# Attention followed by a mixture of experts: the first 128 rows of expert 0 selected by TensorE while the routing still runs

## The chip, the cores and the metric

The kernel runs on one core of a Trainium2 chip. The metric is the device time of one launch in microseconds (us). TensorE is called PE in the profile, VectorE DVE, ScalarE ACT, GpSimd POOL; SP is the engine whose queue starts most of the DMAs.

## The reference

Attention with pooled queries gives 1152 token rows of 512 numbers. A gate chooses one of 8 experts for each token. Expert e takes the first 288 of its tokens in the order of the tokens; each goes through two matrices, 512 to 1024 and 1024 to 512, with a relu between, and the result is scaled by the gate's probability.

```python
q_pool = q.reshape(B, H, S // factor, factor, D).mean(axis=3)       # B, H, S, D = 2, 8, 1152, 64
scores = scale * np.matmul(q_pool, k.transpose(0, 1, 3, 2))
attn = np.exp(scores - np.max(scores, axis=-1, keepdims=True))
attn = attn / (np.sum(attn, axis=-1, keepdims=True) + 1e-09)
x = np.matmul(attn, v).transpose(0, 2, 1, 3).reshape(N, D)          # N, D = 1152, 512
...
expert_idx = np.argmax(x @ w_gate, axis=1)
for i in range(N):
    e = expert_idx[i]
    if counts[e] < capacity:                                        # capacity = 288
        disp[e, counts[e]] = x[i]; pos[i] = counts[e]; counts[e] += 1; keep[i] = True
h = np.maximum(np.einsum('ecd,edf->ecf', disp, w1), 0.0)
y = np.einsum('ecf,efd->ecd', h, w2)
out[i] = gate_w[i] * y[expert_idx[i], pos[i]]                       # for the tokens kept
```

## The kernel before

**Attention.** Eight pairs of heads (four for each of the two batches) go through PE one after the other; a pair has 27 rounds of scores (`s`), exponentials (`p`), transposes (`tp`) and products with the values (`pv`, from a value tile `vraw` that has two buffers). A finished group of a pair is turned into token rows in `x_out` (tile `xps`, then `x_tok` in SBUF and gate products in `lp`). The order on PE is the order in which the code is written; DVE's order in the last rounds is a scheduler's.

**Routing.** `route(b, t0, t1)` works on tiles of 128 tokens. The last batch's tokens come in three pieces: tiles 0 and 1, tiles 2 and 3, and tile 4 (half full). Each piece is some 15 small DVE operations, with two small matmuls on PE between them that count the tokens of the same expert ahead (`rps`). The outcome is `slot`, an integer row number e * 288 + rank for every token. POOL then writes every token row to that row of `xs`, a tensor in device memory, by an indirect DMA (L551, "scatter"), one for each tile of 128 tokens. `classes` counts the tokens of each expert (`cps`) into flags `more_i`, by which the code later branches.

**Filler.** Behind the counts PE has eight matmuls of 128x512 (tile `warm`, L763; the profile shows each as two), whose result nothing uses.

**Experts.** The rows of expert e come back from `xs` into `xe` (`load_x`, L795): expert 0's on SP's queue, the others' on POOL's. `trans_x` turns 128 of them over on PE (`xps`, L802), ACT copies that into `xf` (L803), and a `unit` of 64 places follows: up (`hps`, 32 matmuls, L890), relu, turn over (`htp`), down (`yps`, 32 matmuls, L930), scaling by the gate (`yo`, L822, which needs the gate column that `tags` copies out of `xe` on POOL), and a scatter to the output (L828). An expert with more places has further units of 64, 128 and 32 behind branches (`later`, L950); a branch hint for them is issued behind each up half. `trans_x` of the next expert lies inside the unit. The eight experts run in order on PE.

**Weights.** An expert's weights are four chunks of 1 MB. Sixteen chunk buffers `wraw0` to `wraw15` exist: 0 to 5 from the start, 6 to 15 in memory that attention's tiles leave. SP's queue is in order: chunks 6 to 12, then expert 0's rows, then chunks 13 to 15, and then one for each buffer that comes free.

## Time and profile before

| what | us |
|---|---|
| median of 3 runs (lowest, highest) | 488.81 (488.57, 491.68) |
| profiled execution, its own time | 491.99 |
| its span from the first to the last instruction | 490.3 |
| PE busy in the span | 449.8 |
| mean granted TensorE clock, share of full speed | 0.974 |

The span is 1.7 us shorter than the execution's own time. A time in the profile counts from the span's start. PE is the engine to follow; the other engines' busy shares average over an attention part (up to about 306 us), where all of them work, and an expert part, where PE works nearly alone.

### The profile page before, as it was taken

Reading aid. Unit: us, or ns where it says so; the run is one execution under the profiler, and the core shown is the slowest. Engines: PE = TensorE matmul, PEld = TensorE weight load, DVE = VectorE, ACT = ScalarE, POOL = GpSimd, SP = SyncE. Lnnn points to the kernel's source line nnn. Section 1 sums busy time; section 2 is a strip of 40 time slices with the busy share of each in tenths; the row PEclk is TensorE's granted clock in tenths of the full one; section 3 lists DMA queues with packets and bytes.
Section 4 is the critical chain, followed back from the end, with each engine's and each line's share of the span. In section 5 each row is a group of like instructions: output and inputs, shape, how many; then the busy total and the mean of one; then the engine's idle time right before and its main releaser. Section 6 shows DMA issues by size and latency. Waiting matters only on the chain. (4 is left out here: it accounts for less than half of the span.)

```text
span 490.3 us, 9116 instructions
## 1 busy us (share of the span) xinstructions
PE 449.8 (92%) x3183; PEld 315.5 (64%) x3183; DVE 245.9 (50%) x725; ACT 251.1 (51%) x731; POOL 170.9 (35%) x290
## 2 busy tenths in 40 slices
PE   4779999999999999999999998996999999999990
PEld 3667777777677677677776765464668456674670
DVE  5687777777777999887777565010100011001100
ACT  5777887787787677777777761020221112101100
POOL 4477444344344454454433001522031133112110
PEclk9799999999999999999999999798999999999996
DMA  7998984033043044052104625699983093000000
GB/s 216 276 284 282 385 285 108 5 98 100 5 98 102 1 119 124 3 150 55 30 20 139 260 70 204 215 341 355 363 285 145 5 364 123 13 12 24 12 11 21
DMA packets 55737, 69.96 MB, mean 143 GB/s; under 512 B 21873, under 2 KB 32117, under 8 KB 55680
## 3 DMA queue, kind: packets, MB, share of 16 engines
q1 hardware_dynamic: 50320, 53.56, 35.5%
q0 software_dynamic: 4816, 15.66, 8.5%
q8 instruction: 32, 0.52, 0.4%
q14 instruction: 25, 0.20, 0.1%
q10 hardware_dynamic: 544, 0.02, 0.1%
HBM read 52.48 MB, written 11.98 MB: 131 GB/s over the span
## 5 line engine op out<-in xcount | busy, mean ns | idle before, releaser
L376 DVE TENSOR_REDUCE negm<-s 128x1 f32<-128x384 f32 x216 | 119.6, 554 | 56.9 <-PE s L371 55.8
L371 PE MATMUL s<-k,q 128*128 128x384 f32 x432 | 132.8, 390 | 9.6 <-ACT p L392 9.0
L392 ACT ACTIVATE p<-s,negm 128x384 f32<-128x384 f32 x216 | 125.0, 587 | 14.6 <-DVE negm L380 9.2
L409 PE MATMUL tp<-ident,p 128*128 128x128 f32 x648 | 106.8, 274 | 0.5 <-DVE pt L418 0.4
L371 PEld LDWEIGHTS s<-k,q 128*128 128x128 f32 x432 | 66.8, 194 | 45.3 <-ACT p L392 25.2
L409 PEld LDWEIGHTS tp<-ident,p 128*128 128x128 f32 x648 | 83.9, 141 | 10.0 <-issue 1.4
L420 ACT COPY pt<-tp 128x384 f32<-128x384 f32 (+1 forms) x160 | 69.3, 445 | 38.5 <-PE tp L409 35.5
L434 PE MATMUL pv<-pt,vraw 128*64 128x256 f32 (+2 forms) x612 | 85.4, 403 | 0.8 <-ACT xt L442 0.8
L273 POOL TENSOR_TENSOR q<-qts,q 64x256 fp32r<-64x256 f32 (+1 forms) x76 | 52.0, 693 | 55.0 <-DVE q L267 47.8
L229 POOL TENSOR_TENSOR k<-kts,k 64x384 fp32r<-64x384 f32 x42 | 44.8, 1068 | 53.7 <-DVE k L228 51.9
L890 PE MATMUL hps<-wraw,xf 128*64 128x256 f32 (+1 forms) x448 | 49.7, 390 | 8.1 <-PEq L950 4.6
L828 POOL DMA_INDIRECT out_dram<-yo,id x17 | 17.1, 1006 | 112.9 <-issue 42.5
L434 PEld LDWEIGHTS pv<-pt,vraw 128*64 128x64 f32 x612 | 36.3, 136 | 27.2 <-issue 10.6
L930 PE MATMUL yps<-wraw,ht 128*64 128x256 f32 (+1 forms) x448 | 48.1, 382 | 1.2 <-DVE ht L907 1.2
L895 DVE TENSOR_SCALAR hs<-hps 128x256 f32<-128x256 f32 x12 | 5.1, 425 | 87.9 <-PE hps L890 87.9
L890 PEld LDWEIGHTS hps<-wraw,xf 128*64 128x64 f32 (+1 forms) x448 | 30.5, 136 | 26.5 <-issue 7.5
L392 ACT ACTIVATION_READ_ACCUMULATOR p<-s,negm 128x1 f32 x216 | 44.5, 206 | 0.0
L418 DVE COPY pt<-tp 128x384 f32<-128x384 f32 (+1 forms) x80 | 40.0, 508 | 6.1 <-PE tp L409 6.0
L822 ACT ACTIVATE yo<-yps,gt 128x256 f32<-128x256 f32 (+1 forms) x15 | 7.7, 516 | 61.5 <-PE yps L930 31.1
L930 PEld LDWEIGHTS yps<-wraw,ht 128*64 128x64 f32 (+1 forms) x448 | 28.4, 133 | 16.8 <-ACT ht L909 1.8
L849 PEld LDWEIGHTS hps<-xf,wraw 128*128 128x128 f32 x192 | 21.7, 192 | 1.2 <-issue 1.2
L849 PE MATMUL hps<-xf,wraw 128*128 128x128 f32 x192 | 22.2, 277 | 0.0
(117 smaller groups left out, 377.0 us busy)
## 6 DMA issues: line engine op xcount, KB each, us to landing
wraw<-in_moe_w_dram SPq DMA_DIRECT2D x32, 1024.0 KB, 7.9
vraw<-in_v_dram SPq DMA_DIRECT2D x8, 576.0 KB, 4.0
kc<-k SPq DMA_DIRECT2D x16, 288.0 KB, 4.0
xs<-zrow POOLq DMA_DIRECT2D x4, 1032.0 KB
qraw<-in_q_dram SPq DMA_DIRECT2D x16, 256.0 KB, 3.6
kraw<-in_k_dram SPq DMA_DIRECT2D x14, 288.0 KB, 4.6
xe<-xs POOLq DMA_DIRECT2D x14, 258.0 KB, 6.0
out_dram<-zrow POOLq DMA_DIRECT2D x2, 1024.0 KB
```

What stands on the lines that cost most here:

```text
L229: nc.gpsimd.tensor_tensor(out=tl[rl, c], in0=kt_s[rh, :], in1=f32(tl[rh, c]), op=ALU.subtract)
L273: nc.gpsimd.tensor_tensor(out=tl[r0, 1, c], in0=qt_s[rs, a:z], in1=f32(tl[rs, 0, c]), op=ALU.subtract)
L371: nc.tensor.matmul(ps[:, 0:CW], a, w, start=i == 0, stop=i == len(terms) - 1)
L376: nc.vector.tensor_reduce(out=negm3[g][:, j:j + 1], in_=ps[:, 0:CW], axis=AX.X, op=ALU.max, negate=True)
L392: nc.scalar.activation(pexp[g][:, j * CW:(j + 1) * CW], sthird.pop(n)[:, 0:CW], AF.Exp, bias=negm3[g][:, 3:4], scale=1.0, accum_out=sums[p ...
L409: nc.tensor.transpose(ps[:, i * P:(i + 1) * P], pexp[g][:, kt * P:(kt + 1) * P], ident)
L418: nc.vector.tensor_copy(dst, sr)
L420: nc.scalar.copy(dst, sr)
L434: nc.tensor.matmul(ps[j * D:(j + 1) * D, 0:n], vraw[:, j, kt, :], pts[p, j, src][:, kt, c0:c0 + n], start=kt == 0, stop=kt == KT - 1,)
L849: at = nc.tensor.matmul(ps[:, i * n:(i + 1) * n], raw[c][:, d, i * P:(i + 1) * P], xf[:, d, o:o + n], start=d == 0, stop=d == DC - 1,)
L890: at = nc.tensor.matmul(ps[g * n:(g + 1) * n, 0:256], xf[:, d, o:o + n], raw[c // 512][:, d, c % 512:c % 512 + 256], start=d == 0, stop=d ...
L930: nc.tensor.matmul(ps[k:k + n, 0:256], ht[:, j, g * n:(g + 1) * n], raw[2 + r // 512][:, r % 512 // P, c * 256:(c + 1) * 256], start=i == ...
```

## The change

Expert 0's first 128 rows no longer take the way over `xs` and `xe` to PE. They are made on PE by matmuls with 0/1 matrices:

- DVE compares column numbers 0 to 127 (`col_i`) with a token's `slot` and writes a 128x128 matrix of zeros and ones for each tile of the last batch (`early["sel"]`). A matmul of the token rows (`x_tok`) with it puts each token's row, turned over already, into the column of its place. Tokens of other experts have slots of 288 and more and give columns of zeros.
- The rows that the first batch left in `xs` are loaded into SBUF during the last pair of heads (`load_early`, on SP's queue) and added by a matmul with the identity.
- Both the loaded rows and the 0/1 matrices lie in one tile that takes the buffer of a value tile no longer used.
- `pick` writes the matmuls, four for each tile, into one PSUM tile (`xsel`). The loaded rows and tile 0 come behind round 32 of the last pair, tile 1 behind round 33, tiles 2 to 4 behind the counts. After the last ACT copies the sum to `xf_first`, which the first two units of expert 0 use.
- The eight `warm` matmuls are gone, and so is expert 0's first `trans_x`. Expert 0's rows are still loaded, for gates, row numbers and later units.
- SP loads the first block of expert 1's rows, then expert 0's three, then the rest of expert 1's; POOL keeps experts 2 and up. In unit 0 of expert 0, five empty steps push `trans_x` of expert 1 to the end of the down half, and the flags are read behind the first up half and no more ahead of the unit.

```diff
+    col_i = const.tile([P, P], I32, name="col_i")
+    nc.gpsimd.iota(col_i, pattern=[[1, P]], base=0, channel_multiplier=0)
+    xf_first = const.tile([P, DC, P], F32, name="xf_first")
...
     nc.vector.memset(lp, 0.0)
+    nc.vector.memset(x_tok[MIX:P, B - 1, QT, 0:DM], 0.0)
...
             tc.add_to_no_dep_group("place", ins.ins)
+        if b == B - 1:
+            nc.vector.tensor_tensor(
+                out=early["sel"][:, t0:t1], in0=col_i.unsqueeze(1).to_broadcast([P, nt, P]),
+                in1=slot[:, t0:t1].unsqueeze(2).to_broadcast([P, nt, P]), op=ALU.is_equal,
+            )
...
+    def load_early():
+        t = lt_p.tile([P, 2, KT, D], F32, tag="vraw", name="early", bufs=2).rearrange("p a t d -> p (a t d)")
+        early["x"], early["sel"] = t[:, 0:DM], t[:, DM:DM + NT * P].rearrange("p (t c) -> p t c", c=P)
+        nc.sync.dma_start(out=early["x"], in_=xs[0:P, 0:DM])
+
+    def pick(*which):
+        if "ps" not in early:
+            early["ps"] = s_ps.tile([P, 512], F32, tag="s", name="xsel")
+        ps = early["ps"]
+        for t in which:
+            x, w = (early["x"], ident) if t < 0 else (x_tok[:, B - 1, t, 0:DM], early["sel"][:, t])
+            for d in range(DC):
+                nc.tensor.matmul(
+                    ps[:, d * P:(d + 1) * P], x[:, d * P:(d + 1) * P], w,
+                    start=t < 0 and d == 0, stop=t == QT and d == DC - 1, skip_group_check=True,
+                )
+            if t == QT:
+                nc.scalar.copy(xf_first, ps.rearrange("p (d c) -> p d c", c=P))
...
+        PICK = {32: (-1, 0), 33: (1,)}
...
+                    if p == NP - 1 and i == 12:
+                        load_early()
...
-        routed = classes().ins
-
-
-        warm = m_ps.tile([P, 512], F32, tag="t", name="warm")
-        for _ in range(8):
-            nc.tensor.matmul(warm[:, 0:512], ident, wraw[0][:, 0], start=True, stop=True)
+        with tc.manual_schedule(engines={mybir.EngineType.PE}):
+            classes()
+            pick(2, 3, QT)
...
-    def load_x(e):
-        q = nc.gpsimd if e else nc.sync
-        for s, c in blocks:
+    def load_x(e, part=slice(None)):
+        q = nc.gpsimd if e > 1 else nc.sync
+        for s, c in blocks[part]:
...
-        xf = xfs[e % 2]
+        xf = xf_first if e == 0 and o < P else xfs[e % 2]
...
+        load_x(1, slice(0, 1))
+        load_x(0)
+        load_x(1, slice(1, None))
+        for e in range(2, min(NX, E)):
             load_x(e)
...
-        trans_x(0, 0)
         for e in range(E):
-            nxt = [lambda: trans_x(e + 1, 0), lambda: flags_of(e + 1)] if e + 1 < E else ()
-            unit(e, 0, nxt, hint(e, 1, flags[e]))
+            nxt = [lambda: trans_x(e + 1, 0), lambda: flags_of(e + 1)] if e + 1 < E else []
+            if e:
+                unit(e, 0, nxt, hint(e, 1, flags[e]))
+            else:
+                unit(0, 0, [lambda: None] * 5 + nxt, first_hint)
```

What this makes of the orders, at three places. First PE, from the routing's matmuls to expert 0 (`rps` are the counts of the three pieces, `cps` that of all, `hps` the first up matmul). Before:

```order
L523 MATMUL rps_3901<-oh_3870,upper_69 128x16
L524 MATMUL rps_3901<-tot_2569,ones_72 128x16
L523 MATMUL rps_3942<-oh_3908,upper_69 128x16
L524 MATMUL rps_3942<-tot_3898,ones_72 128x16
L523 MATMUL rps_3955<-oh_3921,upper_69 128x8
L524 MATMUL rps_3955<-tot_3937,ones_72 128x8
L564 MATMUL cps_3982<-tot_3949,ones_72 128x8
L763 MATMUL warm_3989<-wraw0_153,ident_63 128x512 x8
L957 TENSOR_LOAD more_i_100
L802 MATMUL xps_4089<-ident_63,xe0_4042 128x128 x4
L890 MATMUL hps_4099<-wraw0_153,xf0_4045 64x256
```

And after, on the same engine from the same matmul on:

```order
L528 MATMUL rps_3907<-oh_3876,upper_69 128x16
L529 MATMUL rps_3907<-tot_2573,ones_72 128x16
L593 MATMUL xsel_3949<-ident_63,early_3659 128x128 x4
L593 MATMUL xsel_3949<-early_3659,x_tok_107 128x128 x4
L528 MATMUL rps_3958<-oh_3914,upper_69 128x16
L529 MATMUL rps_3958<-tot_3904,ones_72 128x16
L593 MATMUL xsel_3949<-early_3659,x_tok_107 128x128 x4
L528 MATMUL rps_3975<-oh_3927,upper_69 128x8
L529 MATMUL rps_3975<-tot_3944,ones_72 128x8
L574 MATMUL cps_4006<-tot_3965,ones_72 128x8
L593 MATMUL xsel_3949<-early_3659,x_tok_107 128x128 x12
L921 MATMUL hps_4112<-wraw0_157,xf_first_83 64x256
```

Twelve selections stand between the counts of the pieces, twelve behind the last count, and the `warm` matmuls and expert 0's transposes are gone ahead of the first up matmul.

Second DVE, at the slots of the last two pieces (`slot_3910` and `slot_3916` are tiles 2 and 3, the next `slot` is tile 4). Before:

```order
L548 TENSOR_TENSOR slot_3910<-r1_3909 128x2
L532 TENSOR_SCALAR r1_3922<-r1_3922 128x1
L539 TENSOR_SCALAR r1_3922<-r1_3922 128x1
L567 TENSOR_SCALAR cl_3984<-cps_3982 128x8
L533 RECIPROCAL x_tok_104<-r1_3922 128x1
L543 SCALAR_TENSOR_TENSOR slot_3923<-r1_3922 128x1
L567 TENSOR_SCALAR cl_3984<-cps_3982 128x8 x2
L568 CAST more_i_100<-cl_3984 128x24
```

And after:

```order
L553 TENSOR_TENSOR slot_3916<-r1_3915 128x2
L567 TENSOR_TENSOR early_3659<-col_i_81,slot_3916 128x256
L539 TENSOR_TENSOR rt_3926<-rps_3975,oh_3927 128x8
L577 TENSOR_SCALAR cl_4008<-cps_4006 128x8
L543 TENSOR_REDUCE r1_3928<-rt_3926 128x1
L577 TENSOR_SCALAR cl_4008<-cps_4006 128x8
L544 TENSOR_SCALAR r1_3928<-r1_3928 128x1
L577 TENSOR_SCALAR cl_4008<-cps_4006 128x8
L548 SCALAR_TENSOR_TENSOR slot_3929<-r1_3928 128x1
L578 CAST more_i_103<-cl_4008 128x24
L567 TENSOR_TENSOR early_3659<-col_i_81,slot_3929 128x128
```

The comparison for tiles 2 and 3 stands ahead of tile 4's last steps, and tile 4's own is the last operation; the comparison for tiles 0 and 1 stands some twenty rows further up.

Third SP's queue, from chunk 11 to the first chunks of expert 3 (`xe0` and `xe1` are the rows of experts 0 and 1). Before:

```order
L620 DMA wraw11_4037<-in_moe_w2_dram 128x4x512
L620 DMA wraw12_4038<-in_moe_w1_dram 128x4x512
L795 DMA xe0_4042<-xs_68 128x516 x2
L795 DMA xe0_4042<-xs_68 32x516
L620 DMA wraw13_4039<-in_moe_w1_dram 128x4x512
L620 DMA wraw14_4040<-in_moe_w2_dram 128x4x512
```

And after:

```order
L649 DMA wraw11_4066<-in_moe_w2_dram 128x4x512
L649 DMA wraw12_4067<-in_moe_w1_dram 128x4x512
L826 DMA xe1_4072<-xs_68 128x516
L826 DMA xe0_4071<-xs_68 128x516 x2
L826 DMA xe0_4071<-xs_68 32x516
L826 DMA xe1_4072<-xs_68 128x516
L826 DMA xe1_4072<-xs_68 32x516
L649 DMA wraw13_4068<-in_moe_w1_dram 128x4x512
```

One block of expert 1 stands ahead of expert 0's rows now, and two more ahead of chunk 13; further up in the same queue the new load of the first batch's rows stands directly ahead of chunk 6.

## Rows read from the trace of the kernel before

**Rows 1.** The page, busy time and share of the span.

```profile
span 490.3 us, 9116 instructions
PE 449.8 (92%) x3183; PEld 315.5 (64%) x3183; DVE 245.9 (50%) x725; ACT 251.1 (51%) x731; POOL 170.9 (35%) x290
```

**Rows 2.** Timeline, routing to expert 0: start, duration, instructions [idle before, releaser].

```profile
301.63 0.41 DVE L479 TENSOR_TENSOR x_tok<-xps,z 128x256 f32<-128x256 f32 x1
...
301.97 0.17 DVE L473 TENSOR_TENSOR lp<-xps,z 64x16 f32<-64x16 f32 x1
...
303.43 0.15 DVE L548 TENSOR_TENSOR slot<-r 128x2 int32<-128x2 f32 x1
...
304.34 1.02 POOL L551 DMA_INDIRECT xs<-x_tok,slot  x1 [10.90 <-DVE r L512]
...
305.32 10.17 PE L763 MATMUL warm<-wraw,ident 128*128 128x512 f32 x16
...
306.08 0.22 DVE L543 SCALAR_TENSOR_TENSOR slot<-r 128x1 int32<-128x1 f32 x1
...
309.51 0.91 POOL L551 DMA_INDIRECT xs<-x_tok,slot  x1 [0.30 <-issue]
...
311.95 1.29 SPq L795 DMA_DIRECT2D xe<-xs  x3
...
315.33 0.60 PE L802 MATMUL xps<-ident,xe 128*128 128x128 f32 x4
...
315.71 0.18 POOL L812 COPY gt<-xe 64x1 f32<-64x1 f32 x1
...
316.01 0.58 ACT L803 COPY xf<-xps 128x512 f32<-128x512 f32 x1 [11.09 <-PE xps L802]
...
316.65 3.67 PE L890 MATMUL hps<-wraw,xf 128*64 128x256 f32 x32 [0.72 <-ACT xf L803]
```

**Rows 3.** Busy time by stage: PE, PEld, DVE, ACT, POOL, granted clock, DMA share, GB/s.

```profile
302.00:303.00 1.00, 0.20 (x2) 0.10 (x1) 1.00 (x10) 0.00 (x0) 0.00 (x0) 1.00 1.04 401
...
304.00:305.00 1.00, 0.53 (x4) 0.47 (x3) 0.84 (x10) 0.21 (x1) 0.66 (x1) 0.83 0.03 8
...
311.00:312.00 1.00, 1.00 (x3) 0.32 (x2) 0.00 (x0) 0.00 (x0) 0.00 (x0) 0.76 0.18 46
```

**Rows 4.** Timeline of PE alone, experts 0 to 3.

```profile
325.64 3.67 PE L890 MATMUL hps<-wraw,xf 128*64 128x256 f32 x32 [0.69 <-ACTq L950]
...
338.52 5.36 PE L890 MATMUL hps<-wraw,xf 128*64 128x256 f32 x32 [4.58 <-PEq L950]
...
357.33 3.67 PE L890 MATMUL hps<-wraw,xf 128*64 128x256 f32 x32 [0.74 <-ACTq L950]
```

**Rows 5.** The line of the branches, PE's alone: ns min/median/max, first and last start.

```profile
L950 PEldq COMPARE_BRANCH  x19: 65/183/6457, 322.6 to 479.4; - x19
```

**Rows 6.** The line that reads the flags, PE's alone: ns min/median/max.

```profile
L957 PEldq TENSOR_LOAD <-more_i x8: 772/781/1265, 306.7 to 416.4; - x8
```

**Rows 7.** Timeline of SP's DMA issues, the first of chunks 6 and up.

```profile
264.76 1.68 SPq L620 DMA_DIRECT2D wraw<-in_moe_w_dram  x3
```

**Rows 8.** Timeline of PE, the last value products of pair 6.

```profile
275.28 1.83 PE L434 MATMUL pv<-pt,vraw 128*64 128x320 f32 x12
```

**Rows 9.** Busy time by stage in the first pair, columns as in Rows 3.

```profile
26.00:28.00 2.00, 0.67 (x5) 0.61 (x5) 1.93 (x4) 1.37 (x4) 1.85 (x4) 1.00 0.99 350
```

**Rows 10.** Timeline of the start.

```profile
1.99 0.59 DVE L109 MEMSET lp<- 128x640 f32 x1 [0.18 <-issue]
...
4.97 0.76 DVE L200 TENSOR_TENSOR qp<-qraw 128x256 f32<-128x256 f32 x2 [2.38 <-DMA qraw<-in_q_dram]
```

**Rows 11.** DMA issues, KB each, median us to landing.

```profile
xe<-xs POOLq DMA_DIRECT2D x14, 258.0 KB, 6.0
...
xe<-xs SPq DMA_DIRECT2D x2, 258.0 KB, 2.9
```

## The prediction

> **What bounds the kernel now.** I read the page first: PE is busy 92% of the span [rows 1], so only places where PE does nothing useful can give time. Then the timeline from the routing to expert 0 [rows 2], because the change works there and nowhere else. Expert 0's first up matmul starts at 316.65. Followed back: ACT's copy at 316.01, the transposes at 315.33, SP's load of expert 0's rows at 311.95, the fifth scatter at 309.51, the first at 304.34 (five scatters one behind the other, some 1.3 us each), and the last slot, ready at 306.08 + 0.22 = 306.30. PE's rows in this stretch are only filler: 16 `warm` records over 10.17 us. So 316.65 - 306.30 = 10.35 us lie between the moment at which every place is known and the first useful matmul, and nearly all of it is the way over device memory. After 316.65 I read PE alone [rows 4]: the units follow each other with gaps of 0.69 and 0.74 behind a branch, and one of 4.58. No gap there is a wait for weights. So a microsecond won ahead of expert 0 stays won, unless a gap behind it grows.

> The third view is the clock by stage [rows 3]. [...]

> **The change part by part.**

> *Removed: the way over memory.* The last slot, the comparison for tile 4, four matmuls, ACT's copy, then expert 0. No row shows the comparison; the nearest is the 128x256 operation on DVE at 301.63, which takes 0.41 us and lets the next start 0.34 us later [rows 2]. Two comparisons of that width stand ahead of the last slot: 0.68 us if all of it is added, nothing if DVE's waits for PE swallow it. PE's selections ahead of the last counts can hold up those counts by a few tenths more. I take 0.7: last slot at 307.0, with 306.3 and 307.4 as ends. The half-width comparison of tile 4 with its hand-off, 0.3 to 0.4 us, brings PE to 307.4. The last four selections have the shape of the four transposes at 315.33, and from there to the first up matmul the trace shows 316.65 - 315.33 = 1.32 us, ACT's copy included [rows 2]. **At full clock expert 0 starts at 307.4 + 1.32 = 308.7**, 7.95 us earlier. At half clock the twelve selections behind the last count take twice as long, 1.2 us for each four where 0.60 is shown. They can start when tiles 2 and 3 are compared, about 306.4, and end between 308.8 and 310.0; near the lower end, since two groups overlap, 309.1. With the 0.72 us from there to the up matmul **expert 0 starts at 309.8**, 6.85 us earlier.

> *Lost: the filler.* [...] Where `warm` ran, the clock came back 6.2 us after steady work began, a loss of half of that, 3.1 us. Behind the 4.58 us gap the up half took 5.36 us and not 3.67, a loss of 1.69 us [rows 4]. I take the middle, 2.4.

> *Moved: the next expert's transposes* go to the end of expert 0's down half, so ACT's 0.58 us copy now stands directly ahead of `yo`, on whose end PE's next unit waits (the 0.69 us gap is released by ACT's queue [rows 4]). Part of it overlaps the last matmuls; I charge 0.2 us, with 0 and 0.58 as ends.

> *Moved: the flag load.* It now sits between the up halves of expert 0 on PE. It takes 772 ns at least [rows 6], but for the other experts it already lies inside the down half, which takes the same 3.67 us as an up half without one; nothing, and 0.8 us if that cover fails.

> *Moved on SP.* The new load waits for pair 6's last value products, which end at 275.28 + 1.83 = 277.1 [rows 8]. Behind it in the queue stand chunks 6 and up, now issued from 264.76 [rows 7]; they start 12 us later. Expert 1 needs chunk 6 only after 317, so this costs nothing; were it to cost, PE would show a wait in expert 1's down half. The three more issues ahead of chunk 13 are 0.43 us each (three in 1.29 us [rows 2]); expert 3 starts at 357.33 [rows 4]. Nothing. Expert 1's first block leaves first, lands 2.9 us behind 311.95 [rows 11], and is wanted around 316 at the earliest.

> *Added at the start.* A memset on DVE like the 0.59 us one there lies ahead of a wait of 2.38 us for the first load [rows 10]; a small GpSimd table likewise. Nothing.

> **The sum.** With the clock at half: 6.85 - 2.4 - 0.2 = 4.25 us. The profiled execution took 491.99 us and would take 487.7; against the median of 488.81, 3.2 us lower, the same difference gives **484.6**. With the clock at full: 7.95 - 0.2 = 7.75 us, **481.1**.

> **The rivals.**

> *The clock stays at full* (481.1). For it: the new matmuls fall into the idle microseconds, and in the first pair PE was busy only 0.67 of 2 us at one place, still at full clock [rows 9]. Against it: tiles 0 and 1 have 12 matmuls of 0.15 us, under 2 us of work, for a stretch from 302 to 306.4, and about 1.5 us of it (between the loaded rows' selection and that of tile 0, which needs the comparison) stays empty; stretches as empty as before made it fall. Its own limit is the gate: `yo` would be wanted at 317, and expert 0's block, second on SP's queue at 312.4, lands 2.9 to 6.0 us later [rows 11] with about 0.6 us of POOL's copies behind it. Up to 2 us can be lost to that, hence 481.1 to 483.1. In the half-clock case `yo` is wanted later than that.

> *A jump without its code* (slower). PE's branch instruction takes 65 to 183 ns as a rule, and 6457 ns once [rows 5]; that is the 4.58 us gap behind expert 1 [rows 4]. It came while the DMA engines were full of weights. The change lets PE reach the jump behind expert 0 some 4 to 8 us earlier, shortly behind a hint that now waits for the first up half, and while row blocks and chunk 13 are on their way. If that jump stalls too, it costs 4.58 - 0.69 + 1.69 = 5.6 us: 484.6 + 5.6 = **490.2**. The point from which it decides is 4.25 us of stall. By the same arithmetic the stall that is there may go, **479.0**; nothing in the change aims at that.

> [...]

> *It comes to nothing* (488.8): the selection starts late because something on PE or DVE holds it, and expert 0 starts where it did. I see no wait that could do so.

> **How the numbers follow.** Half clock 0.45, full clock 0.35, a stalled jump more 0.12, the old stall gone 0.05, nothing 0.03. The likeliest gives 484.6; its own range, with the ends of its terms, is 483 to 486. The range for 8 in 10 takes in full clock with the comparisons hidden (480.4) and the case of nothing, and leaves out the two about stalls: 480.0 to 489.0. One per cent is 4.9 us, about what a measurement of this kernel can tell from no change. Faster by more (under 483.9): full clock, the stall gone and a quarter of the half-clock case, 0.52. Slower by more (over 493.7) needs a stalled jump and the worst clock: 0.06. Within: 0.42.

> **What would show it.** The first up matmul of expert 0 between 308.5 and 310; the granted clock from 304 to 316, and that up half between 3.7 us (full) and 7.3 (half); no scatter in front of expert 0 on the chain; five scatters where they were; `yo` of expert 0 behind POOL's gate copy or not; one PE branch of several us, or two, or none. I am wrong if PE waits for the comparisons far beyond 307.4, or if the gaps behind expert 0 grow by what was won.

## The result, and the profile after

The change made the kernel slower where it was first timed: 495.27 us (494.69 to 496.30, four runs) against 490.14 us for the kernel before, ratio 1.0106 [1.0075, 1.0137]. 484.6 was predicted, within 480.0 to 489.0. The same kernel on another chip (e5 below) took 491.12 against 491.48, ratio 1.0015 [0.998, 1.0051]. Medians are of all runs of a kernel; ratios and their intervals leave out the few slow runs, over 1.5% above the same kernel's fastest. Between the two timings lies mostly one jump, as will be seen; a gain is in neither.

The page of the changed kernel: span; PE's busy time; the queue q8 with its packets, MB and share; and the group of the up matmuls, with busy time and mean ns, then idle time ahead of it and what ended most of that.

```profile
span 492.9 us, 9183 instructions
PE 445.1 (90%) x3211; PEld 315.7 (64%) x3211; DVE 246.3 (50%) x729; ACT 251.6 (51%) x731; POOL 170.0 (34%) x288
...
q8 instruction: 34, 0.56, 0.5%
...
L921 PE MATMUL hps<-wraw,xf 128*64 128x256 f32 (+1 forms) x416 | 47.6, 398 | 12.9 <-PEq L981 11.6
```

PE does less (445.1 us busy, 449.8 in [rows 1]: `warm` is gone) in a longer span. The last line says where the time went: 11.6 us in which PE waited for its own sequencer at a branch. In [rows 4] that was one gap of 4.58.

The timeline from the routing to expert 0, which answers [rows 2]:

```profile
299.38 1.15 PE L469 MATMUL xps<-wgi,xt 128*128 128x144 f32 x6
...
300.29 0.41 DVE L484 TENSOR_TENSOR x_tok<-xps,z 128x256 f32<-128x256 f32 x1
...
305.11 0.25 PE L574 MATMUL cps<-tot,ones 128*128 128x8 f32 x1
...
305.53 2.05 PE L593 MATMUL xsel<-early,x_tok 128*128 128x128 f32 x16 [0.17 <-DVE early L567]
...
306.62 0.17 DVE L539 TENSOR_TENSOR rt<-rps,oh 128x8 f32<-128x8 f32 x1 [1.14 <-PE cps L574]
...
307.20 0.22 DVE L548 SCALAR_TENSOR_TENSOR slot<-r 128x1 int32<-128x1 f32 x1
...
307.46 0.29 DVE L567 TENSOR_TENSOR early<-col_i,slot 128x128 f32<-128x128 int32 x1
307.80 0.97 PEld L593 LDWEIGHTS xsel<-early,x_tok 128*128 128x128 f32 x8 [0.41 <-DVE early L567]
307.81 1.16 PE L593 MATMUL xsel<-early,x_tok 128*128 128x128 f32 x8 [0.22 <-DVE early L567]
...
310.40 0.59 ACT L598 COPY xf_first<-xsel 128x512 f32<-128x512 f32 x1 [6.77 <-PE xsel L593]
```

Expert 0 starts at 311.04, and its rows no longer come over device memory. Measured from `x_tok` on DVE, since the attention ended 1.3 us earlier in this execution, that is 10.75 us where it was 15.02. What to see here: four selections take 1.16 us, in eight records, where the four transposes took 0.60; and twice a reader of PE's results starts 1.3 to 1.4 us behind the matmuls' end as the trace gives it (DVE at 306.62, with the counts `cps`, whose end released it, over at 305.36; ACT at 310.40, with the last selections over at 308.97).

PE alone behind that, which answers [rows 4], and the line of the branches, which answers [rows 5]:

```profile
325.00 6.54 PE L921 MATMUL hps<-wraw,xf 128*64 128x256 f32 x32 [4.92 <-PEq L981]
...
337.49 3.67 PE L921 MATMUL hps<-wraw,xf 128*64 128x256 f32 x32 [1.32 <-PEq L981]
...
356.04 3.67 PE L921 MATMUL hps<-wraw,xf 128*64 128x256 f32 x32 [1.66 <-PEq L981]
...
404.58 2.13 PE L921 MATMUL hps<-wraw,xf 128*64 128x256 f32 x17 [3.75 <-PEq L981]
```

```profile
L981 PEldq COMPARE_BRANCH  x19: 65/182/6328, 318.4 to 482.2; - x19
```

Each of the four rows starts behind a taken jump over an expert's unused bodies: behind experts 0, 1, 2 and 4. Before, only that behind expert 1 had such a gap. The account of the two executions, as differences between starts (before from [rows 1, 2, 4]):

| stretch | before | after | change |
|---|---|---|---|
| start to `x_tok` | 301.63 | 300.29 | -1.34 |
| `x_tok` to expert 0 | 15.02 | 10.75 | -4.27 |
| expert 0 to expert 1 | 8.99 | 13.96 | +4.97 |
| expert 1 to expert 2 | 12.88 | 12.49 | -0.39 |
| expert 2 to expert 3 | 18.81 | 18.55 | -0.26 |
| expert 3 to the end | 132.97 | 136.86 | +3.89 |
| span | 490.3 | 492.9 | +2.6 |

What was won ahead of expert 0 is gone at the next jump, and the stretch that holds the one behind expert 4 takes 3.9 more.

### The profile page after: what moved, and what is told of

It reads as the page before. It is cut to its first block, busy times and chain, and to the rows that moved or that the text cites. A ratio compares the mean times of both kernels' runs of the same rounds, so it can differ in the third digit from the quotient of the medians.

```text
span 492.9 us, 9183 instructions
## 1 busy us (share of the span) xinstructions
PE 445.1 (90%) x3211; PEld 315.7 (64%) x3211; DVE 246.3 (50%) x729; ACT 251.6 (51%) x731; POOL 170.0 (34%) x288
## 5 line engine op out<-in xcount | busy, mean ns | idle before, releaser
L376 PE MATMUL s<-k,q 128*128 128x384 f32 x432 | 131.3, 387 | 9.8 <-ACT p L397 9.4
L921 PE MATMUL hps<-wraw,xf 128*64 128x256 f32 (+1 forms) x416 | 47.6, 398 | 12.9 <-PEq L981 11.6
L928 ACT ACTIVATE hs<-hps 128x256 f32<-128x256 f32 x14 | 5.4, 385 | 33.8 <-PE hps L921 31.7
```

The lines of the kernel that those rows point to most:

```text
L376: nc.tensor.matmul(ps[:, 0:CW], a, w, start=i == 0, stop=i == len(terms) - 1)
L921: at = nc.tensor.matmul(ps[g * n:(g + 1) * n, 0:256], xf[:, d, o:o + n], raw[c // 512][:, d, c % 512:c % 512 + 256], start=d == 0, stop=d ...
```

## The experiments

Three theories. **1:** whether a jump stalls depends on where the experts' code stands in PE's program, and the change moved it: 24 selections in, 8 `warm` and 4 transposes out, 56 PE instructions more ahead of expert 0. **2:** the jumps stall because the change reaches them earlier and behind a later hint. **3:** the jumps wait for code that is fetched, and the fetches queue behind row and weight loads that the change moved. That a stalled jump waits for its code was the author's supposition; no run shows it. Of the queue that the page calls q8 `instruction` the pages show its size: 32 packets and 0.52 MB before, 34 and 0.56 MB after.

One table serves all runs: ns of PE's branch behind experts 0, 1, 2, 4 and 5 (x0 to x5), median, and ratio to the kernel before, measured beside it. "Shift" is by how many instructions the branch behind expert 4 stands further on in PE's built program than in the kernel before.

```
run                      shift    x0    x1    x2    x4    x5  median  ratio
before                       0  2232  6457   367  1031  2529
after                       55  6328  3205  3290  5634  1748  495.27  1.0106 [1.0075, 1.0137]
e1_before_shifted           56  4903  4731  1570  6292  1592  497.36  1.0158 [1.0101, 1.0215]
e2_after_unshifted           1   390  4663   351   880  3392  485.48  0.9893 [0.9857, 0.9928]
e3_early_flag               55   395  5269  3164  5566  1724  490.87  0.9988 [0.9946, 1.0031]
e4_ahead_1                  55   387  5769   351  5177  1690  490.90  0.9989 [0.9956, 1.0023]
e5_after_again              55   484  4233   936  5948  1679  491.12  1.0015 [0.9980, 1.0051]
e6_after_dead_code         254  2721  4907   351   946  3318  488.92  0.9956 [0.9923, 0.9989]
e7_early_flag_dead_code    254  2492  4758   349  1019  3358  489.83  0.9935 [0.9902, 0.9968]
e8_early_flag_dead_96      150  2508  4927  2762  1291  3115  487.56  0.9899 [0.9850, 0.9949]
f1_filler_both             256   390  5134   349   601  2412  484.74  0.9866 [0.9808, 0.9923]
f2_no_hints                236  6974  6022   334  6223  3308  497.96  1.0103 [1.0065, 1.0142]
f3_before_shifted_back     255  4790  2535   360   453  3614  492.36  1.0028 [0.9997, 1.0060]
f4_after_filler             65   387  4788  2804  5931  1457  492.03  0.9989 [0.9952, 1.0026]
g1_filler_both_again       256  1761  6378   362   436  3350  488.16  0.9926 [0.9888, 0.9964]
g2_late_flag_filler        256  1864  6618   362   951  3888  489.66  0.9950 [0.9923, 0.9977]
g3_earlier_hint            261   395  4309   349   975  3307  484.08  0.9820 [0.9770, 0.9869]
h1_before_earlier_hint       5  2147  6413   367   354  3560  489.61  0.9907 [0.9864, 0.9950]
h2_after_earlier_hint       60   395  2909  1684  5586  1604  487.72  0.9924 [0.9893, 0.9955]
h3_fastest_again           261   390  4029   352  1072  3552  482.21  0.9802 [0.9756, 0.9849]
```

In all these profiles the branch starts 1.7 to 2.4 us ahead of PE's gap, while PE still works at earlier matmuls; of each branch over 2.6 us all but 1.3 to 2.0 us shows as idle PE time (6328: 4.92; 3205: 1.32).

### The place of the code, without the change, and the change without the shift

```diff
 # e1, in the kernel before
-        for _ in range(8):
-            nc.tensor.matmul(warm[:, 0:512], ident, wraw[0][:, 0], start=True, stop=True)
+        for _ in range(22):
+            nc.tensor.matmul(warm[:, 0:184], ident, wraw[0][:, 0, 0:184], start=True, stop=True)
 # e2, in the changed kernel's pick()
             for d in range(DC):
+                if t in (0, 1, 2) or t == 3 and d < 2:
+                    continue
```

> The kernel before, with its 8 warm matmuls of 512 columns cut into 22 of 184: nearly the same columns, but 14 more calls, each of which is two MATMUL and two LDWEIGHTS records, so that all code of the experts stands 56 PE instructions later in the program, as the change puts it. Nothing else of the change is in it. Theory 1 (which jumps stall depends on where the experts' code stands in the program, and the change shifted it): the four idle stretches released by PE's sequencer appear as in the changed kernel, behind experts 0, 1, 2 and 4, and the time goes up by about 10 us, the 5 that the changed kernel lost and the 5 that it had won ahead: 497 to 503. Theory 2 (the jumps stall because the change brings PE to them earlier and behind a later hint): as the kernel before, 489 to 492, one such stretch behind expert 1. Theory 3 (the code fetches queue behind row and weight loads that the change moved): the same 489 to 492.

> The changed kernel with 14 of its 24 selections left out (those of tiles 0, 1 and 2 and half of tile 3, so that rows of expert 0 from these tiles are missing from its output). The last tile, its wait and ACT's copy stay, so expert 0 starts when it did; the experts' code stands where the kernel before has it. Theory 1: the stall behind expert 0 goes, one of some 4.6 us behind expert 1 is back, those behind experts 2 and 4 shrink to 0.7: 484 to 487. Theory 2: the stalls stay where the changed kernel has them, 493 to 497. Theory 3: the same 493 to 497.

Measured: 497.36 and 485.48. Fourteen matmul calls more, under the scatters' cover, cost the kernel before 1.6%. The changed kernel with fourteen fewer took 1.1% less than the kernel before; it leaves out part of expert 0's rows, so it is a test and no version to use. PE in the first:

```profile
326.58 5.36 PE L890 MATMUL hps<-wraw,xf 128*64 128x256 f32 x32 [2.91 <-PEq L950]
...
339.41 3.67 PE L890 MATMUL hps<-wraw,xf 128*64 128x256 f32 x32 [2.84 <-PEq L950]
...
357.28 3.67 PE L890 MATMUL hps<-wraw,xf 128*64 128x256 f32 x32 [0.67 <-ACTq L950]
...
406.48 5.33 PE L890 MATMUL hps<-wraw,xf 128*64 128x256 f32 x32 [4.41 <-PEq L950]
```

The gaps behind experts 0 and 4 are there without any of the change's other parts, and the up half behind these two takes 5.36 and 5.33 us for 3.67, as behind the 4.58 us gap of the kernel before (5.36 [rows 4], with a granted clock of 0.50 from 340 to 342). Behind expert 2 the branch lengthened too (1570), but no PE gap shows. Theory 1 is borne out for expert 4, and the two others have no room for it there: e1 has neither the change's hint nor its loads. For expert 0 it is not shown: of the seven profiles with the code shifted this way (shift 55 to 65) five have only 387 to 484 ns there.

### Hint and loads

```diff
 # e3: flags_of(0) ahead of the experts, and
-                unit(0, 0, [lambda: None] * 5 + nxt, first_hint)
+                unit(0, 0, [lambda: None] * 5 + nxt, hint(0, 1, flags[0]))
 # e4
-AHEAD = 2
+AHEAD = 1
```

> The changed kernel with expert 0's flag load ahead of the experts and a branch hint behind both of its up halves, as the kernel before has them. Theory 1: the stall behind expert 0 stays, 493 to 498. Theory 2: PE's branch behind expert 0 falls from 6328 ns to under 200 and the time to 488 to 491.

> The changed kernel with one expert weight load fewer let go at a time on SP's queue (AHEAD 1 in place of 2). Theory 3: the fetches of code meet fewer transfers, the stalled branches shorten and the time falls below 492. Theories 1 and 2: the stalls stay where they are, 494 to 498; loads may now come late.

> The changed kernel itself once more, beside the three that follow, since its first timing had four runs on another chip. Theory 1 (the place of the experts' code in the program decides which jumps stall): 493 to 497, branches of several us behind experts 1 and 4 at least. Theory 2 (the late hint): the branch behind expert 0 is again over 4 us. If both the stall behind expert 0 and the 1.4 us wait of ACT's copy for PE were accidents of the one execution, the copy follows the last selection at once, that branch is under 1 us, and the median is 490 to 492, as the two kernels with one line changed (early flag, AHEAD 1) had it.

Both small edits gave 490.9, and the branch behind expert 0 fell to 395 and 387 ns; that looked like theories 2 and 3 at once. But the changed kernel itself, run again, had 484 there and 491.12. Of the thirteen executions compared six took 490.2 to 491.2 and seven 494.2 to 496.4. PE in e5, behind experts 0 and 4 (4.92 and 3.75 us of gap in the profile after):

```profile
320.55 3.67 PE L921 MATMUL hps<-wraw,xf 128*64 128x256 f32 x32 [0.95 <-ACTq L981]
...
398.72 6.59 PE L921 MATMUL hps<-wraw,xf 128*64 128x256 f32 x32 [4.07 <-PEq L981]
```

So in one and the same program the jump behind expert 0 stalls in some executions and not in others. Neither edit is shown to decide it, and what does stays open. The branch behind expert 4 stayed at 5.2 to 5.9 us in all three, as theory 1 has it.

### Code that never runs

```diff
 # e6, in later(): expert 0 has at most 64 tokens here, so this body isn't entered
+            if e == 0 and u == 1:
+                ps = tr_ps.tile([P, 512], F32, tag="tr", name="dead")
+                for _ in range(50):
+                    nc.tensor.matmul(ps[:, 0:P], ident, ident, start=True, stop=True)
 # e7: the same in e3; e8: the same with 24 calls
```

With the change's own instructions the 199 of e6 make a shift of 254, and e8's 24 calls one of 150. That a shift of 254 would be as good as none was the author's estimate. The forecast for e8 is of the branch behind expert 1, 5269 ns in e3.

> The changed kernel with 50 matmul calls (199 PE instructions) added in the body of expert 0 that runs only if it has more than 64 tokens, which it hasn't: they are never executed. [...] Theory 1: the branches behind experts 2 and 4 are again under 1100 ns (after: 3290 and 5634), that behind expert 1 stays at 4 us or more, and the time is 4 us below the changed kernel of the same job. Theories 2 and 3: dead code changes nothing, within 1 us of it.

> As the run with expert 0's flag and hints as before, with the same 199 instructions that never run. Theory 1: the long branches behind experts 2 and 4 (3164 and 5566 there) go, that behind expert 1 stays: 490.9 - 4.5 = 486.4, between 485 and 488, below both kernels. Theories 2 and 3: 490 to 492, as without the dead code.

> [...] If what counts is the distance from the last jump or the load on the DMA queues, behind expert 1 it stays over 4 us: 489 to 492.

> The kernel before with warm cut into 22 calls, as in the first run (497.4 there), and 50 calls that never run in expert 0's second body, so that experts 1 to 7 stand 256 instructions behind their place in the kernel before. Nothing of the change is in it. Theory 1 (the place of the code): the branches behind experts 2 and 4 are short again (1570 and 6292 there) and the time comes back to 490 to 493. If the 22 calls themselves cost the time, it stays at 496 to 499.

Instructions that are never executed took the branch behind expert 4 from 5948 to 946 ns and that behind expert 2 from 936 to 351; in e6:

```profile
336.02 5.36 PE L921 MATMUL hps<-wraw,xf 128*64 128x256 f32 x32 [3.02 <-PEq L981]
...
354.83 3.67 PE L921 MATMUL hps<-wraw,xf 128*64 128x256 f32 x32 [0.74 <-ACTq L981]
...
400.29 3.67 PE L921 MATMUL hps<-wraw,xf 128*64 128x256 f32 x32 [0.67 <-ACTq L981]
```

The time was 2.2 us below that of the changed kernel measured with it (e5), not 4, and e7 missed its 485 to 488: both lost 1.6 to 1.7 us in the first up half (see the filler, below). f3 undid most of e1's loss with the same 22 calls in place (ratio 1.0028 after 1.0158), so the calls themselves were not the cost. Over the table, the branch behind expert 4 takes 5177 to 6292 ns in all seven profiles at a shift of 55 to 65, and 354 to 1291 in the twelve others with hints. The branch behind expert 5 goes the other way: 1457 to 1748 ns in the seven, 2412 to 3888 in the twelve, so one move of the code helps one jump and hurts another. The branch behind expert 4 was short at a shift of 0 (1031), again at 254 and 255 (946 in e6, 453 in f3), and also at e8's 150 (1291). Expert 1's took 4927 ns in e8, over 4 us as its forecast has it, but the time was 487.56 and not 489 to 492. Only shifts of 0 to 5, 55 to 65, 150 and 254 to 261 were tried with hints, and why the place matters stays open.

### The hints

```diff
 # f2, in e7 with 52 calls
-            return lambda: tc.mark_branch_hint_location(f"u{e}_{u}", hint=flags[u - 1], engines=ENG)
+            return lambda: None
 # g3, in g1: one hint more, ahead of the first up half; h1: the same in the kernel before; h2: in e3
+        if u == 0:
+            hint()
```

> As the run with the early flag and 50 calls that never run (52 here), with all branch hints left out, on every engine. If the hints bring the code of a jump's target ahead of it, every taken jump of PE now takes over 4 us, that behind expert 4 too (1019 ns there): 500 or more. If they do little on PE, the jumps take what they took, 488 to 491.

> The first one with one hint more for each expert, ahead of its first up half, 1.3 us or more before those there. If the branch behind expert 1 (5134 ns there, 3.25 us of PE's idle time) waits because its hint comes too late, it shortens by 1 us or more and the time falls to 482 to 485. If something else keeps its code from coming, it stays at 4 us or more and the time is that of the first, within 1 us.

Without hints three of the five jumps, not all as the first branch of the forecast had it, take 6 to 7 us: those of experts 0, 1 and 4 (6974, 6022 and 6223 ns; 2492, 4758 and 1019 in e7). Those of experts 2 and 5 take 334 and 3308, about what they took with hints (349 and 3358 in e7). f2's shift, 236, was not tried with hints, so how much of this is the hints and how much the place is not shown.

With one hint more, earlier, the gap behind expert 1 was 2.52 us (g3). The same program without it had 4.50 in one profile (g1) and 3.25 in another (f1), and in the kernel before the hint left that branch where it was (6413 ns in h1, 6457 before), so a shorter stall there is not shown to be its work. Something else came that was not looked for. The page's span and the timeline's last scatter of g1, then of g3:

```profile
span 487.5 us, 9189 instructions
...
478.11 0.98 POOL L866 DMA_INDIRECT out_dram<-yo,id  x1 [13.64 <-ACTq L988]
```

```profile
span 484.2 us, 9221 instructions
...
477.51 0.98 POOL L866 DMA_INDIRECT out_dram<-yo,id  x1 [13.64 <-POOLq L990]
```

From the scatter's start to the end it is 9.4 us in the one and 6.7 in the other. The hints are POOL's instructions too, and it is 6.7 to 7.0 us in f2, h1, h2 and h3 as well, every kernel with another number of hints, and 9.3 to 9.5 in before, after and g1. Why was not tried apart.

### Filler in the routing

The 1.4 us by which ACT started behind the selections were not in every profile. In e4, with the same PE program:

```profile
299.87 1.15 PE L469 MATMUL xps<-wgi,xt 128*128 128x144 f32 x6
...
300.77 0.42 DVE L484 TENSOR_TENSOR x_tok<-xps,z 128x256 f32<-128x256 f32 x1
...
306.01 2.94 PE L593 MATMUL xsel<-early,x_tok 128*128 128x128 f32 x24 [0.17 <-DVE early L567]
...
309.00 0.59 ACT L598 COPY xf_first<-xsel 128x512 f32<-128x512 f32 x1 [4.88 <-PE xsel L593]
```

From `xps` to the copy it is 9.13 us here and 11.02 in the profile after. Filler tests whether that is the clock:

```diff
 # f1 (in e7, 48 calls that never run), f4 (in the changed kernel), g1 = f1, g2 = f1 with the late flag
+            if t == 0:
+                keep_busy(384)     # nc.tensor.matmul(ps[:, 0:384], ident, wraw[0][:, 0, 0:384])
...
                 nc.scalar.copy(xf_first, ps.rearrange("p (d c) -> p d c", c=P))
+                keep_busy(256)
```

> As the run with the early flag and 50 calls that never run (48 here), with two matmul calls whose result nobody reads: one of 384 columns between the selections of the loaded rows and those of tile 0, where PE waits about 1 us for the comparison, and one of 256 columns behind the last selection, under ACT's copy. Theory A (the routing's PE work runs partly at half clock, though the recorded clock stays at full: that would explain 1.9 us more from the last xps to the copy in five of seven profiles, and the fall of the recorded clock behind it): the copy starts 9.1 us behind the last group of xps and not 11.0, the first up half takes 3.67 us, 486 to 488. Theory B (PE's results were held back by something else, such as POOL's scatters): copy at 11.0 us, 489 to 490.5.

> The changed kernel with the two matmul calls whose result nobody reads, and nothing else (8 PE instructions more ahead of the experts, so the branch behind expert 4 stays long). Theory A: copy 9.1 us behind the last xps, first up half 3.67 us; executions near 489 where expert 0's jump doesn't stall and 493 where it does. Theory B: copy at 11.0 us, 491 to 495 as the changed kernel.

> The fastest version so far once more (early flag, two filler calls, 48 calls that never run; 484.7 against 491.7). If filler keeps the clock up in the routing, the copy starts again 9.1 us behind the last group of xps and the first up half takes 3.67 us; 483 to 487. If that was chance, the copy is at 11.0 us with odds of about five in eight and the time 1 to 4 us more.

> The same with expert 0's flag load and single place of hints as the change has them. Theory 2 (late hint): the branch behind expert 0 takes over 4 us in some executions, median 487 to 491. If with the code moved the late hint costs nothing: the branch under 600 ns, 483 to 487.

f1 and f4 had 9.12 us and looked like proof, and f1 was the fastest so far with the whole output (484.74). g1, the same program, had 10.92 and missed its 483 to 487 (488.16); g2 had 10.87, g3 10.95. So filler doesn't remove these 1.8 us. All changed kernels that were measured together agree (9.1 with e3 and e4, with f1, f2 and f4, and with h2 and h3; 10.9 to 11.0 with e5 to e8 and with g1 to g3). What it is stays open; the recorded granted clock is 1.00 from 300 us to the copy in the profile after, in e4 and in e6.

The first up half took 3.67 us in all six profiles with filler, and 5.24 to 6.40 in four of the ten without (e2, e6, e7, e8). That filler did this is not shown: f2 and h2, without it, have 3.67 too, beside kernels that have it. In e6 the wait of 2.08 us behind the selections is followed by a stretch at a granted clock of 0.50, here its first row and one microsecond of it (length, PE busy, granted clock, DMA share, GB/s):

```profile
312.60 5.36 PE L921 MATMUL hps<-wraw,xf_first 128*64 128x256 f32 x32 [2.08 <-ACT xf_first L598]
...
314.00:315.00 1.00, 1.00 (x8) 0.50 1.09 400
```

That is 1.7 us, the "lost filler" of the prediction, in some executions. The late flag (g2) costs nothing that these runs tell: 1864 against 1761 ns at expert 0, and overlapping intervals.

### The change's own worth, with the code back in its place

> The kernel before with one hint more for each expert, ahead of its first up half, and nothing of the change. If the hint shortens the stall behind expert 1 (4.58 us of idle time before) by 1 to 2 us and the POOL wait at the end (2.7 us) goes as in the fastest run, 491 - 4 = 487, between 485 and 489, and the change itself adds only 3 us to that in the fastest version. If the hint works only together with the change, 490 to 492.

> The changed kernel with the early flag and the hint ahead of each first up half; no filler, no code that never runs, so the code stands where the change put it. Theory 1 (place of the code): the branch behind expert 4 is still over 4 us; with 2.0 us won behind expert 1 and 2.7 at the end, 486 to 489. If hints that come early enough make the place indifferent, that branch too is under 1.5 us: 481 to 485.

> The fastest version once more (filler, early flag, hint ahead, code that never runs; 484.1 against 491.0): 482 to 486, with 8.3 us from the last matmul to the end, and branches behind experts 2 and 4 under 1100 ns.

h3, with filler, early flag, one hint more and 48 calls that never run, is faster than both kernels: 482.21 us, ratio 0.9802 [0.9756, 0.9849], after 0.9820 for the same program in g3. h1 is the kernel before with the same hint, and its branch behind expert 4 is as short at a shift of 5 (354 ns) as h3's at 261 (1072); it gains 0.9%. h2, without filler and moved code, keeps its long branch behind expert 4 (5586), as theory 1 says, and its ratio is not told from h1's. PE in h1, then in h3:

```profile
324.70 3.67 PE L890 MATMUL hps<-wraw,xf 128*64 128x256 f32 x32 [0.69 <-ACTq L952]
...
337.63 5.17 PE L890 MATMUL hps<-wraw,xf 128*64 128x256 f32 x32 [4.63 <-PEq L952]
```

```profile
310.07 3.67 PE L928 MATMUL hps<-wraw,xf_first 128*64 128x256 f32 x32 [0.24 <-ACT xf_first L604]
...
314.69 3.24 PE L970 MATMUL yps<-wraw,ht 128*64 128x256 f32 x28
317.87 0.66 PE L840 MATMUL xps<-ident,xe 128*128 128x128 f32 x4
318.45 0.65 PE L970 MATMUL yps<-wraw,ht 128*64 128x256 f32 x4
320.06 3.67 PE L928 MATMUL hps<-wraw,xf 128*64 128x256 f32 x32 [0.95 <-ACTq L990]
...
330.60 5.36 PE L928 MATMUL hps<-wraw,xf 128*64 128x256 f32 x32 [2.25 <-PEq L990]
```

Their ratios to the kernel before lie 1.05% apart, some 5 us, and the intervals do not touch; the medians of all runs lie 7.4 us apart. Expert 0 starts 5.63 us earlier in h3 (at 315.70 in h1), expert 1 4.64, expert 2 7.03. The 2.4 us between the last two are a shorter gap behind expert 1 (2.25 for 4.63). They are not shown to be the change's. The branch there takes 2909, 4029 and 4309 ns in the three profiles that have the change and this hint and 6413 in h1, but over all profiles it goes from 2535 to 6618, h1's profile is of an execution of 490.78 us where others of the same kernel took 483.5 to 485.5, and nothing in the change aims at that jump. So what these two profiles show for the change is the 4.6 us at the start of expert 1.

## Why the prediction was wrong

**The step that failed** is the sentence that closes the reading: no gap is a wait for weights, "so a microsecond won ahead of expert 0 stays won, unless a gap behind it grows". Gaps grew at once, by what was won, which is the prediction's own last sign of being wrong: 4.27 us were won up to expert 0, and 4.97 were lost from there to expert 1 and 3.89 behind expert 3. The rival "a jump without its code" named such a stall, and the jump behind expert 0, but that a jump stalls for want of its code is shown by no run; it priced one more stall at 5.6 us, gave it 0.12 and tied it to time (reaching the jump sooner, a later hint, loads on their way). For the jump behind expert 4 the runs put the place of the code in its stead. For the one behind expert 0, some 4.0 of the 4.97 us (13.96 in the profile after, 9.99 in e5), they show only that the same program has it in some executions (6328 ns) and not in others (484); its cause stays open.

The part on the change counted what each added instruction costs while it runs, and not that it moves what stands behind it: 56 instructions ahead of expert 0 decide over the branch behind expert 4 (e1, e2, e6, f3), and in six of seven profiles go with a longer one behind expert 2. The built program gave the count of added instructions and the profile the jumps behind them; the question what the one does to the other was not asked, and a range that stopped at 489 left the case out. The row of the branches was misread as well: 65 and 183 ns are the shortest and the median of 19 [rows 5], and the same profile has 2232, 1031 and 2529 ns behind experts 0, 4 and 5 (first row of the table), with PE gaps of only 0.69, 0.67 and 0.67 us. So at least four of PE's 19 branches, not one, took over 1 us before the change.

**Start of expert 0.** Forecast 7.07 us behind `x_tok` at full clock (308.7 - 301.63); 10.75 in the profile after, 8.86 in e4. Of the 1.8 us that are missing in the better case, about 1.1 are the selections, 2.94 us for twelve calls where 1.80 follows from the price: they are two records each, the transposes one. The road was another one, too. The sum went by the last slot, the comparison for tile 4 and four selections; in e4 PE ran all twelve without a pause (306.01 to 308.95) and waited for neither, though the slot came 0.5 us later than taken. The twelve started 5.24 us behind `x_tok` where "about 306.4" means 4.77, which is 0.5 us, and the sum's own start and price for twelve give 308.9 and not 308.7, which is the rest. The other 1.9 us, in the profile after, are the open wait of the routing.

**The clock.** Half clock was put ahead of full, at 2.4 us. That is the author's middle of two estimates; no run shows a loss of 2.4 us there. In the kernel before the granted clock was 0.50 from 305 to 311 us, with PE busy 0.38 of the 2 us from 302 to 304. In the profile after PE was busy 1.15 of those 2 us, the clock was 1.00 from 300 to 320, and the first up half took 3.67. In four of ten profiles without filler it took 1.6 to 2.7 us more; in e6, the one of them with the clock read, it was 0.50 from 314 to 316, behind the same 2.08 us of idle PE as in the profile after. So half clock was neither the likeliest case nor one with one price.

**The next expert's transposes** were charged at 0.2 us and cost 1.0: from expert 0 to expert 1 it is 9.99 us in h3 where it was 8.99 [rows 2, 4]. 0.26 is the gap (0.95 for 0.69), about as priced. The rest was forgotten: in the old place the transposes lay where PE otherwise waits for `hs` (0.22 us ahead of the second `htp` in h3), and the down half behind them was one piece. Before:

```profile
320.53 0.60 PE L802 MATMUL xps<-ident,xe 128*128 128x128 f32 x4
320.96 0.38 PE L904 MATMUL htp<-ident,hs 128*128 128x128 f32 x2
321.28 3.67 PE L930 MATMUL yps<-wraw,ht 128*64 128x256 f32 x32
```

In the new place they stand inside the down half, which takes 4.41 us in h3 (314.69 to 319.10), 0.74 more.

**Right:** the clear road past memory (no scatter in front of expert 0), SP's order, chunks 6 and up, the memsets, and the flag load at no cost that shows. Against the full-clock case, 7.95 - 0.2 = 7.75 us, h3 and h1 show 5.63 at the start of expert 0 less 1.0 for the transposes, 4.6.

## What to carry to other kernels

In this program 56 instructions added ahead of the jumps had a price that has nothing to do with what they do (e1: ratio 1.0158; the branch behind expert 4 6292 ns for 1031). Where a program jumps over code, compare the long branches of both profiles before anything else, and try the old kernel with the same number of idle instructions added. Instructions that never run were a cheap way here to move code back (expert 4's branch 5948 to 946 ns from e5 to e6), though the place that was good for one jump was bad for another (expert 5's 1679 to 3318). Do not take a difference seen in one profile for the work of the edit until the same program has been profiled twice; twice here such a theory fell.
